# Chunked attention and a two-layer block in one kernel: dense weights, whole turns, grouped scores and values, transposes by the DMA crossbar, and W1 scaled in place

## The chip, the core and the metric

The kernel runs on one core of a Trainium2 chip. The core has a matrix engine (TensorE, PE in the profile; its weight loads are the row PEld), a vector engine (VectorE, DVE), a scalar engine (ScalarE, ACT), GpSimd (POOL) and a queue for transfers (SyncE, SP). TensorE writes to PSUM, eight banks of 2 KB per partition; the other engines copy from there to SBUF. Transfers are issued by an engine's queue and carried out by 16 DMA engines. The metric is device microseconds of one execution; lower is better. Each engine works through its own instructions in order and waits where an input is not there.

## What is computed

Four batches of eight heads, 768 positions, head width 64. Each chunk of 32 queries looks at 8 memory keys, up to 16 keys before the chunk, its own 32 and 8 behind. The heads side by side give 512 numbers per position, and on these runs a normalised two-layer block with a residual:

```python
k_full = np.concatenate([mem_k, k_ctx], axis=2)
v_full = np.concatenate([mem_v, v_ctx], axis=2)
scores = scale * np.matmul(q_c, k_full.transpose(0, 1, 3, 2))
scores = scores - np.max(scores, axis=-1, keepdims=True)
a = np.exp(scores)
a = a / (np.sum(a, axis=-1, keepdims=True) + 1e-09)
out[:, :, c_start:c_end] = np.matmul(a, v_full)
...
xn = (x - mu) / np.sqrt(var + 1e-06) * g_ln
ch = np.maximum(xn @ w_ch1, 0.0) @ w_ch2
return (x + ch).astype(np.float32)
```

w_ch1 is 512 x 2048, w_ch2 is 2048 x 512.

## The kernel before

Work is cut into 24 tiles of 128 positions (tile t is batch t // 6) and 12 pairs of tiles (pair u is tiles 2u and 2u+1). A tile is four chunks of 32 queries: two groups (`gg`) of 64, each with two chunks (`y`). For one tile the attention goes like this, with the lines of the profile:

- `qk` (L313): `qk_products` makes 32 small products (L294) in one PSUM bank. Each has 64 contraction rows (one head; two heads, `par`, lie in the two halves of the partitions), 32 queries and 64 keys. `below_max` (L304, L305, DVE) takes off the row maximum, `weights` (L311, ACT) the exponential into `P`.
- `pt` (L317): four TensorE transposes (L321) turn `P`, and two copies (L330), first DVE for one half of the partitions and then ACT for the other, put it into `PTz`. There each half of the partitions (keys of chunk y) holds only its own chunk's queries; the other places are zeros, set once.
- `val` (L367): `val_products` has 16 products (L336) of 128 contraction rows, 64 queries and 65 columns (values and a column of ones) in the two banks `two`. The zeros make one product serve both chunks. `tokens` (L345, L346, L352, DVE) divides by the sum and gives the mean; `shift` (L359 on POOL, L363 on ACT in the first six tiles) takes the mean off into `xn`.
- `root` (L374 on ACT, L378 and L382 on POOL) makes the inverse deviation `rstd`, used only at the end, when the result is added.
- `turn_x` (L388): four TensorE transposes of `xn`; a DVE copy (L394) multiplies by `g` on the way into `xT`.

For a pair, `up` (L407) has eight blocks of 8 products of 256 columns, each block followed by a ReLU copy (L415 on ACT) into `rT`. The second layer is `down` (L423, eight blocks of four products of 512 columns) in pairs 0 and 1, and from pair 2 on `down7` (L472): seven blocks of 8 products of 256 columns, by sums of blocks of the weights (`w2_sum`, L453, into `T`) and of `rT` (`r_sum`, L468). After each, DVE adds into `xs` (L479), and SP stores a finished tile (L433, L484).

Keys and queries of a batch come by POOL transfers into `raw`, heads apart: `turn` (L232) makes 16 narrow transposes of 96 rows for two heads, and copies (L245, L252) put the result into `KT` and `QD`. Memory keys are put into `KT` by `mem_cols`. Values come by POOL transfers straight into `V` (`load_v_group` L125 and L130 for batch 1, `load_v_head` L139 and L144 after it, `load_v_ends`); SP makes the copies inside `V` that chunks share (`v_shared` L161, `v_mem` L166).

The order is written out by hand; no scheduler moves anything. Batch 0 and pairs 0 and 1 are straight code. From pair 2 on, `plan` lists for pair u and step 0 to 15 what is put in ahead of that step's block: even steps are `up` of pair u, odd steps `down7` of pair u-1 (`down` in pair 2; none at step 15). While pair u runs, the attention of the two tiles of pair u+1 is made: scores at steps 0 and 2, `pt` at 4 and 7, `val` at 6 and 9, `turn_x` at 11 and 14 (in pair 2 all but the turns are four steps later; turns at 14 and 16). Batches 2 and 3 are turned in pairs 3 and 4, and 6 and 7, four turns a pair, at steps 8, 9, 12 and 13; their loads are issued at step 5 of pairs 2 and 5.

PSUM banks that are free for turns and scores go round through `slot()`: from pair 2 on there are only two of them, `one`.

Of the kernel before, what the change touches and what calls it, by code (L numbers as in the profile page):

```python
# [9 lines left out]
FP16 = mybir.dt.float16  # L10
# [6 lines left out]
def kernel(  # L17
# [50 lines left out]
    PTz = [sb.tile([128, 16, 2, 32], FP16, name=f"PTz{i}") for i in range(3)]  # L68
# [187 lines left out]

    RAW = ((0, 1), (0, 1), (2, 0), (1, 2))

    def turn_k(b, j, engine):
        to_stream(KT[b % 2], turn(raw[RAW[b][0]], 2 * j), j, engine)  # L260

    def turn_q(b, j, engine):
        to_rows(b, turn(raw[RAW[b][1]], 2 * j), j, engine)
# [53 lines left out]
    def pt(t, engines="VA"):  # L317
# [8 lines left out]
        z = PTz[t % 3]  # L326
        src = pv.rearrange("p (c q) -> p c q", c=16)
        for y in range(2):
            rows = slice(64 * y, 64 * y + 64)
            copy_on(engines[y])(out=z[rows, :, y, :], in_=src[rows, :, :])  # L330

    def val_products(t):
        b, tt = t // 6, t % 6
        for h in range(H):
            for gg in range(2):
                nc.tensor.matmul(  # L336
                    out=two[64 * gg : 64 * gg + 64, 128 * h : 128 * h + 65],
                    lhsT=PTz[t % 3][:, 4 * (h // 2) + 2 * gg + h % 2, :, :],
                    rhs=V[b % 2][:, 2 * tt + gg, h, 0:65],
                    start=True, stop=True, tile_position=(0, 64 * gg),  # L340
                )
# [42 lines left out]
    def turn_x(t):  # L384
        p = slot()
        pv = as16(p)[:, 0:512]
        for dt in range(4):
# [6 lines left out]
        nc.vector.tensor_tensor(  # L394
            out=xT[(t // 2) % 3][:, :, 128 * i : 128 * i + 128],
            in0=pv.rearrange("p (d c) -> p d c", d=4),
            in1=free(g_col, 0, [[1, 4], [0, 128]]), op=ALU.mult,
        )

# [196 lines left out]
    for i in range(2):  # L596
        nc.vector.memset(PTz[i][64:128, :, 0, :], 0.0)
        nc.vector.memset(PTz[i][0:64, :, 1, :], 0.0)
# [10 lines left out]
    nc.vector.memset(PTz[2][64:128, :, 0, :], 0.0)  # L609
    nc.vector.memset(PTz[2][0:64, :, 1, :], 0.0)  # L610
# [29 lines left out]
    shift(1, "A")  # L640
    turn_x(0)
# [18 lines left out]
    for g in range(2):  # L660
        load_v_group(1, g)
    up(0, 3)
# [16 lines left out]
    v_turn(7, "A")  # L679
    up(0, 4)  # L680
# [34 lines left out]
    banks["list"] = one + upb  # L715
    down(0, 0)
    val(5, "A")
    turn_x(4)
    down(0, 1)
    mem_cols(KT[1], memKT[:, 4:8, :], True)  # L720
    down(0, 2)
    turn_x(5)
    down(0, 3)
    root(4)
    for g in range(6, 9):
        load_v_group(1, g)
    turn_k(1, 0, "V")
    down(0, 4)
    root(5)
    for g in range(9, NG):  # L730
        load_v_group(1, g)
    turn_k(1, 1, "A")
    down(0, 5)
    turn_k(1, 2, "V")
    down(0, 6)
    turn_k(1, 3, "A")
# [12 lines left out]
    for j in range(4):  # L749
        at(2, j, turn_q, 1, j, "AV"[j % 2])  # L750
    for u in range(2, NP - 1):
        a, c = 2 * u + 2, 2 * u + 3
        d = 4 if u == 2 else 0
        at(u, d, qk, a)
        at(u, d + 2, qk, c)
        at(u, d + 4, pt, a)
        at(u, d + 6, val, a)
        at(u, d + 7, pt, c)
        at(u, d + 9, val, c)
        if u == 2:  # L760
            at(u, 14, turn_x, a)
            at(u, 15, root, a)
            at(u, 16, turn_x, c)
            at(u, 16, root, c)
        else:
            at(u, 11, turn_x, a)
            at(u, 12, root, a)
            at(u, 14, turn_x, c)
            at(u, 14, root, c)
# [4 lines left out]
    for b in range(2, B):  # L774
        u0 = 3 * b - 3
        at(u0 - 1, 5, load_kq, b)
        for j in range(4):
            w, s = u0 + j // 2, 8 if j % 2 == 0 else 12
            at(w, s, turn_k, b, j, "V")
            at(w, s + 1, turn_q, b, j, "A")  # L780
        for h in range(H):
            for part in range(2):
                at(u0, 2 * h, load_v_head, b, h, part)
        at(u0 + 1, 0, load_v_ends, b)
        at(u0 + 1, 8, v_shared, b, 0, NG)
# [58 lines left out]
```

## Time and profile before

| What | Value |
| --- | --- |
| Runs | 255.0, 256.27, 256.6 us; median 256.27 |
| Profiled execution, first to last instruction (span) | 255.3 us; the page gives no other time for it |
| Mean granted TensorE clock | 0.971 |
| Busy: PE, DVE, ACT, POOL | 235.8, 176.0, 122.0, 94.4 us |
| Start, to the first `up` of pair 0 | 28.7 us |
| Pair 0; 1; 2 | 22.4; 19.0; 19.1 us |
| Pairs 3, 4, 5, 6 | 19.1, 19.05, 16.15, 18.6 us |
| Pairs 7, 8, 9, 10 | 19.0, 16.1, 16.6, 16.7 us |
| Pair 11 and the last `down7` | 20.4 us |
| Last stores | 4.3 us |

The page has busy times per engine, a strip of the span in 40 slices, the chain of work that ended last, groups of instructions by line, and transfers by name. Beside it the trace was read in order of time and by stretches. In the order of time a row is: start, length, engine, line, operation, output<-inputs, tile sizes, count, and in brackets how long the engine stood idle before it and for whom. PE products overlap, so a row's length is more than its share; the distance from one start to the next is what counts.

### The profile page before, as it was taken

What the parts mean: (1) busy time and instruction counts of PE and PEld (TensorE: products, weight loads), DVE (VectorE), ACT (ScalarE), POOL (GpSimd) and SP (SyncE); (2) the same over time, 40 slices, a digit from 0 to 9 for tenths busy, and PEclk for the clock granted to TensorE, in tenths of its full rate; (3) what the DMA queues carried; (4) which work ended last, traced back from release to release, by engine and by line L of the source; (5) the groups of instructions that cost most, each with busy time, mean ns of one, the idle gap of its engine ahead of it and who ended that gap; (6) DMA issues with size and microseconds to landing.
All of it is one profiled execution on the core that took longest, in us unless ns stands there. A gap on an engine that the chain in (4) does not pass through costs nothing.

```text
span 255.3 us, 8286 instructions
## 1 busy us (share of the span) xinstructions
PE 235.8 (92%) x3611; PEld 192.9 (76%) x3611; DVE 176.0 (69%) x390; ACT 122.0 (48%) x226; POOL 94.4 (37%) x164
## 2 busy tenths in 40 slices
PE   8697978999999989999999999999999999999983
PEld 7353656786566778888789878878889888899972
DVE  7535574757597598697696687687775966856272
ACT  2225456578345445545644464554555444653310
POOL 8394332016991296741322638712113022121000
PEclk9959995999999999999999999999999999999999
DMA  6989999932999987974196569933101002011022
GB/s 82 139 94 207 208 215 206 202 27 17 60 172 143 198 103 46 103 101 70 65 155 114 104 42 58 135 70 61 57 3 51 34 3 82 3 43 43 3 82 83
DMA packets 45816, 23.50 MB, mean 92 GB/s; under 512 B 33492, under 2 KB 41140, under 8 KB 45732
## 3 DMA queue, kind: packets, MB, share of 16 engines
q0 software_dynamic: 40672, 14.70, 49.2%
q1 hardware_dynamic: 5108, 8.28, 11.1%
q8 instruction: 28, 0.46, 0.8%
q14 instruction: 8, 0.07, 0.1%
HBM read 29.46 MB, written 6.29 MB: 140 GB/s over the span
## 4 chain that ended last, share of the span: by engine, by line
PE 69%; DVE 18%; ACT 4%; DMA 4%; issue 3%; DVEq 0%; ACTq 0%; POOLq 0%
PE upb L407 28%; PE dnb L472 18%; PE dnb L423 5%; DVE RS L468 4%; PE one L232 4%; DMA raw<-in_k_dram 4%; PE two L336 4%; DVE nmx L304 3%; DVE sub L305 3%; DVE xs L479 3%; PE one L294 2%; PE one L388 2%; ACT PTz L330 2%; PE upb L542 2%; DVE T L453 1%
## 5 line engine op out<-in xcount | busy, mean ns | idle before, releaser
L407 PE MATMUL upb<-xT,w1c 128*128 128x256 f16 x768 | 101.3, 276 | 1.2 <-DVE xT L394 0.9
L407 PEld LDWEIGHTS <-w1c 128*128 128x128 f16 x768 | 80.0, 115 | 5.5 <-DVE xT L394 1.4
L415 ACT ACTIVATE rT<-upb 128x512 f16<-128x512 f32 x92 | 54.6, 593 | 56.9 <-PE upb L407 56.7
L479 DVE SCALAR_TENSOR_TENSOR xs<-dnb,rstd,xs 128x256 f32<-128x256 f32 x70 | 33.7, 481 | 24.3 <-PE dnb L472 23.1
L359 POOL TENSOR_SCALAR xn<-xs,nmean 128x512 f16<-128x512 f32 x18 | 12.4, 691 | 76.6 <-DVE nmean L352 36.8
L472 PEld LDWEIGHTS <-RS 128*128 128x128 f16 x320 | 30.0, 98 | 4.3 <-DVE RS L468 0.7
L311 ACT ACTIVATE P<-sub 128x512 f16<-128x512 f32 x24 | 15.2, 632 | 35.0 <-DVE sub L305 34.9
L472 PE MATMUL dnb<-T,RS 128*128 128x256 f16 x240 | 30.9, 273 | 0.8 <-DVE xs L479 0.8
L472 PEld LDWEIGHTS <-rT 128*128 128x128 f16 x240 | 23.1, 98 | 2.6
L472 PE MATMUL dnb<-w2c,rT 128*128 128x256 f16 x160 | 20.6, 273 | 0.0
L394 DVE TENSOR_TENSOR xT<-one,g_col 128x512 f16<-128x512 f16 x22 | 15.1, 687 | 7.4 <-PE one L388 7.2
L232 PEld LDWEIGHTS <-raw 96*64 96x64 f16 (+2 forms) x576 | 13.5, 110 | 8.6 <-issue 5.8
L378 POOL TENSOR_SCALAR veps<-ssq 128x1 f32<-128x1 f32 x24 | 5.4, 227 | 36.2 <-ACT sq L374 36.0
L374 ACT ACTIVATE sq<-xs,nmean 128x512 f16<-128x512 f32 x24 | 17.3, 719 | 0.2
L346 DVE CUSTOM_DVE_ANT_1 xs<-two,rec 128x512 f32<-128x512 f32 x24 | 16.6, 691 | 0.8
L468 DVE TENSOR_TENSOR RS<-rT 128x1024 f16<-128x1024 f16 x20 | 13.7, 686 | 4.9 <-ACT rT L415 4.9
L423 PE MATMUL dnb<-w2c,rT 128*128 128x512 f16 x64 | 16.3, 380 | 0.0
L336 PEld LDWEIGHTS <-PTz 128*64 128x64 f16 x384 | 8.5, 114 | 10.2 <-ACT PTz L330 6.0
L304 DVE TENSOR_REDUCE nmx<-one 128x8 f32<-128x512 f32 x21 | 14.4, 684 | 2.1 <-PE one L294 2.0
L305 DVE TENSOR_TENSOR sub<-one,nmx 128x512 f32<-128x512 f32 x21 | 14.5, 691 | 0.7
L336 PE MATMUL two<-V,PTz 128*64 128x65 f16 x384 | 11.1, 202 | 4.1 <-ACT PTz L330 3.3
L382 POOL TENSOR_TENSOR rstd<-veps,mhalf 128x1 f32<-128x1 f32 x24 | 13.3, 554 | 2.0
(118 smaller groups left out, 321.4 us busy)
## 6 DMA issues: line engine op xcount, KB each, us to landing
out_dram<-xs SPq DMA_DIRECT2D x23, 256.0 KB, 2.0
raw<-in_k_dram POOLq DMA_DIRECT2D x4, 768.0 KB, 9.8
raw<-in_q_dram POOLq DMA_DIRECT2D x3, 768.0 KB, 14.8
w1c<-in_moe_w_ch_dram POOLq DMA_DIRECT2D x2, 1024.0 KB, 13.3
w2c<-in_moe_w_ch_dram POOLq DMA_DIRECT2D x4, 512.0 KB, 22.7
V<-in_v_dram POOLq DMA_DIRECT2D x16, 77.0 KB, 3.1
V<-in_v_dram POOLq DMA_DIRECT2D x15, 56.0 KB, 4.1
V<-memv SPq DMA_DIRECT2D x6, 120.0 KB
```

The costliest lines, as they stand in the source:

```text
L232: nc.tensor.matmul(out=pv[64 * par : 64 * par + 64, n * r : n * r + n], lhsT=src[lo : lo + n, heads + par, r, :], rhs=identity[lo : lo + n ...
L304: nc.vector.tensor_reduce(out=m, in_=scores, axis=AX.X, op=ALU.max)
L305: nc.vector.tensor_tensor(out=s.rearrange("p (c k) -> p c k", c=8), in0=scores, in1=free(m, 0, [[1, 8], [0, 64]]), op=ALU.subtract,)
L336: nc.tensor.matmul(out=two[64 * gg : 64 * gg + 64, 128 * h : 128 * h + 65], lhsT=PTz[t % 3][:, 4 * (h // 2) + 2 * gg + h % 2, :, :], rhs=V ...
L346: nc.vector.tensor_tensor_reduce(out=x.rearrange("p (h d) -> p h d", h=H), in0=free(two, 0, [[128, 8], [1, 64]]), in1=free(r, 0, [[1, 8], ...
L374: nc.scalar.activation(out=sq, in_=xs[t % 9], func=ACTF.Square, bias=nmean[t % 6], scale=1.0, accum_out=ssq[i],)
L407: nc.tensor.matmul(out=p[:, 256 * hb : 256 * hb + 256], lhsT=free(w1c[hc // 8][:, dt, :], 512 * (hc // 4 % 2) + hc % 4, [[4, 128]]), rhs=x ...
L415: nc.scalar.activation(out=o, in_=i, func=ACTF.Relu)
L423: nc.tensor.matmul(out=p, lhsT=rT[u % 2][:, hc, 128 * i : 128 * i + 128], rhs=w2c[hc // 4][:, hc % 4, :], start=(hc == 0), stop=(hc == 15),)
L468: nc.vector.tensor_tensor(out=RS[k], in0=a, in1=b, op=op)
L472: nc.tensor.matmul(out=p[:, 0:256], lhsT=left[:, n, :], rhs=right(n), start=(n == 0 and not add), stop=(n == 7), skip_group_check=add,)
L479: nc.vector.scalar_tensor_tensor(out=x, in0=p[:, 0:256], scalar=rstd[t % 9], in1=x, op0=ALU.mult, op1=ALU.add,)
```

## The change

- **Dense weights.** `PTz` is replaced by `PT`, the turned weights as they are. One copy by ACT instead of two halves. `val_products` makes 32 products of 64 contraction rows and 32 queries, each half of the partitions by itself.
- **Whole turns.** From batch 1 on, POOL's new `mix` copies two heads side by side (96 x 1024), and `turn_mixed` turns 96 x 128 in 8 products instead of 16. Keys and queries of batch 1 are turned in pair 1 (one query turn in pair 2), those of batches 2 and 3 all in pairs 3 and 6; their loads are issued at step 0 of the pair before.
- **Crossbar.** From tile 8 on, weights and tokens are turned by transposing DMAs on SP's queue: `cross_p` from `P` to `PT` (no PSUM, no copy), `cross_x` from `xn` to `xT`.
- **Grouping.** From pair 3 on, `val` of tile t and the scores of tile t+2 stand together, at steps 4 and 8; `cross_x` at 6 and 10, `cross_p` at 7 and 11, `root` at 7 and 11.
- **W1 times g.** `scale_w1` multiplies W1 by `g` in place, in eight passes of 128 x 1024 (five on DVE, three on ACT); the copy after `turn_x` is a plain one.
- **Moved.** `w2_sum` 0 and 1 to pair 1, 2 and 3 to steps 7 and 9 of pair 2; `mem_cols` of batches 1 to 3 earlier; V loads of batches 2 and 3 from step 0 to step 6 of pairs 3 and 6 on, and the V copies two steps later.

```diff
-    PTz = [sb.tile([128, 16, 2, 32], FP16, name=f"PTz{i}") for i in range(3)]
+    PT = [sb.tile([128, 4, 128], FP16, name=f"PT{i}") for i in range(3)]
+    mixed = [sb.tile([128, 8, 128], FP16, name=f"mixed{i}") for i in range(4)]
...
+    def mix(b, which, j):
+        src, m = raw[RAW[b][which]], mixed[(2 * j + which) % 4]
+        nc.gpsimd.tensor_copy(
+            out=m[0:96, :, :].rearrange("p r (a d) -> p r a d", a=2),
+            in_=free(src[0:96], 1024 * j, [[64, 8], [512, 2], [1, 64]]),
+        )
+    def turn_mixed(which, j):
+        p, src = slot(), mixed[(2 * j + which) % 4]
+        pv = as16(p)
+        for r in range(8):
+            nc.tensor.matmul(
+                out=pv[:, 96 * r : 96 * r + 96], lhsT=src[0:96, r, :],
+                rhs=identity[0:96, 0:96], is_transpose=True, start=True, stop=True,
+            )
+        return pv
...
-        z = PTz[t % 3]
-        src = pv.rearrange("p (c q) -> p c q", c=16)
-        for y in range(2):
-            rows = slice(64 * y, 64 * y + 64)
-            copy_on(engines[y])(out=z[rows, :, y, :], in_=src[rows, :, :])
+        copy_on(engine)(out=PT[t % 3].rearrange("p j q -> p (j q)"), in_=pv)
...
-                nc.tensor.matmul(
-                    out=two[64 * gg : 64 * gg + 64, 128 * h : 128 * h + 65],
-                    lhsT=PTz[t % 3][:, 4 * (h // 2) + 2 * gg + h % 2, :, :],
-                    rhs=V[b % 2][:, 2 * tt + gg, h, 0:65],
-                    start=True, stop=True, tile_position=(0, 64 * gg),
-                )
+                for y in range(2):
+                    rows, col = slice(64 * y, 64 * y + 64), 64 * gg + 32 * y
+                    q0 = 64 * gg + 32 * (h % 2)
+                    nc.tensor.matmul(
+                        out=two[col : col + 32, 128 * h : 128 * h + 65],
+                        lhsT=PT[t % 3][rows, h // 2, q0 : q0 + 32],
+                        rhs=V[b % 2][rows, 2 * tt + gg, h, 0:65],
+                        start=True, stop=True, tile_position=(64 * y, col),
+                    )
...
+    def cross_x(t):
+        i = t % 2
+        nc.sync.dma_start_transpose(
+            out=xT[(t // 2) % 3][:, :, 128 * i : 128 * i + 128], in_=xn[t % 3],
+        )
+    def cross_p(t):
+        nc.sync.dma_start_transpose(out=PT[t % 3], in_=P[t % 3])
+    def scale_w1(c, dt, engine):
+        w = w1c[c][:, dt, :]
+        if engine == "A":
+            nc.scalar.activation(out=w, in_=w, func=ACTF.Copy, scale=g_col[:, dt : dt + 1])
+        else:
+            nc.vector.tensor_scalar(
+                out=w, in0=w, scalar1=g_col[:, dt : dt + 1], scalar2=None, op0=ALU.mult,
+            )
...
     shift(1, "A")
+    for dt in range(4):
+        scale_w1(0, dt, "AV"[dt // 2])
     turn_x(0)
...
     v_turn(7, "A")
+    for dt in range(4):
+        scale_w1(1, dt, "VVVA"[dt])
     up(0, 4)
...
+            for step, t in ((4, a), (8, c)):
+                at(u, step, val, t)
+                if t + 2 < 2 * NP:
+                    at(u, step, qk, t + 2)
+            at(u, 7, root, a)
+            at(u, 11, root, c)
+            at(u, 6, cross_x, a)
+            if u < NP - 2:
+                at(u, 7, cross_p, a + 2)
+            at(u, 10, cross_x, c)
+            if u < NP - 2:
+                at(u, 11, cross_p, c + 2)
...
-        at(u0 - 1, 5, load_kq, b)
+        at(u0 - 1, 0, load_kq, b)
+        for n, (j, which) in enumerate((j, w) for j in range(4) for w in range(2)):
+            w, step = ((-1, 12), (-1, 13), (0, 0), (0, 1), (0, 3), (0, 5), (0, 6), (0, 7))[n]
+            at(u0 + w, step, mix, b, which, j)
+            step = (1, 2, 5, 6, 10, 11, 13, 15)[n]
...
         for h in range(H):
+            w, step = divmod(6 + 2 * h, 16)
             for part in range(2):
-                at(u0, 2 * h, load_v_head, b, h, part)
+                at(u0 + w, step + part, load_v_head, b, h, part)
```

## The prediction

> **What bounds the kernel now.** I read the page's busy times, clock row and chain first, then TensorE in order of time, then the stages, then DMA and POOL. Busy share, clock and chain agree:
>
> ```profile
> PE 235.8 (92%) x3611; PEld 192.9 (76%) x3611; DVE 176.0 (69%) x390; ACT 122.0 (48%) x226; POOL 94.4 (37%) x164
> ...
> PEclk9959995999999999999999999999999999999999
> ...
> PE 69%; DVE 18%; ACT 4%; DMA 4%; issue 3%; DVEq 0%; ACTq 0%; POOLq 0%
> ```
>
> TensorE is full from 28.7 us to the tail at full clock, except near 38 to 45 us (tenth 5). So from pair 1 on, a microsecond of TensorE work is a microsecond of time, unless another engine is late. What one block costs is the distance between starts in the order of time (ends are modelled), here inside pair 7:
>
> ```profile
> 162.14 0.41 PE L294 MATMUL one<-KT,QD 64*32 64x64 f16 x32
> 162.48 1.07 PE L407 MATMUL upb<-xT,w1c 128*128 128x256 f16 x8
> 163.39 1.04 PE L472 MATMUL dnb<-w2c,rT 128*128 128x256 f16 x8
> ...
> 166.47 0.39 PE L321 MATMUL one<-identity,P 128*128 128x128 f16 x4
> 166.70 1.04 PE L407 MATMUL upb<-xT,w1c 128*128 128x256 f16 x8
> 167.57 1.04 PE L472 MATMUL dnb<-T,RS 128*128 128x256 f16 x8
> 169.19 0.44 PE L336 MATMUL two<-V,PTz 128*64 128x65 f16 x16 [0.58 <-ACT PTz L330]
> 169.56 1.07 PE L407 MATMUL upb<-xT,w1c 128*128 128x256 f16 x8
> 170.47 0.39 PE L321 MATMUL one<-identity,P 128*128 128x128 f16 x4
> 170.69 1.04 PE L472 MATMUL dnb<-T,RS 128*128 128x256 f16 x8
> 171.66 0.53 PE L232 MATMUL one<-identity,raw 96*64 96x96 f16 x16
> 172.12 1.07 PE L407 MATMUL upb<-xT,w1c 128*128 128x256 f16 x8
> ```
>
> An `up` or `down7` block takes 0.87 (166.70 to 167.57); turning the weights 0.23 (166.47 to 166.70), the tokens 0.22. Scores take 0.35 and values 0.37, but a full-array block ahead of such a narrow one takes 0.97, and the block behind 0.91: changing the shape costs 0.14, so 0.49 and 0.51. A narrow turn takes 0.46 + 0.13 = 0.59. In the row at 169.19 values also wait 0.58 for ACT's half of the weights' copy, which starts only after DVE's half. The stages:
>
> ```profile
> 89.20:108.30 19.10, 18.11 (x298) 15.56 (x296) 15.56 (x33) 10.42 (x21) 14.38 (x24) 1.00 0.86 85
> ...
> 162.14:181.18 19.04, 18.13 (x297) 15.57 (x296) 14.76 (x35) 10.18 (x19) 5.92 (x11) 1.00 0.44 73
> 181.18:197.30 16.12, 15.94 (x232) 14.28 (x232) 12.14 (x28) 8.09 (x16) 2.56 (x7) 1.00 0.09 34
> ```
>
> (Stretch and its length, then busy PE, PEld, DVE, ACT, POOL, clock, DMA.) Pairs with turns take about 19 us, those without 16 to 16.7; pairs 3 to 10, 89.2 to 230.6, together 141.4.
>
> **Pairs 3 to 10.** Old contents per pair: 15 blocks x 0.87 = 13.1, two scores 0.98, two values 1.02, two weight and two token turns 0.90; sixteen narrow turns lie in pairs 3, 4, 6, 7. That is 8 x 16.0 + 16 x 0.59 = 137.4; the other 4.0 are waits like the 0.58 above and the 0.94 for xT at 90.56. The change:
> - Turns of weights and tokens leave TensorE for tiles 8 to 23: 16 x 0.45 = -7.2.
> - Whole turns: 8 products of 96 columns instead of 16. Scaled from the 128-column turn (0.23 for four), 0.34; at the same time per product, 0.46. I take 0.38, with no change of shape: 16 x 0.21 = -3.4.
> - Values: 32 products instead of 16, each half as tall and half as wide. The scores have just this form (64 rows, 32 columns, two row halves into one bank) and run at 0.34/32 = 11 ns, so 0.35 against 0.37: I take nothing. Upper end: 23 ns each, as the old values ran, +0.37 a tile.
> - Grouping: values and the next-but-one scores stand together in one shape, 14 changes of 0.14 gone: -2.0; two scores move to pair 2: -0.7.
> - The 4.0 of waits: weights are now ready a pair early and the end-of-pair token turn is gone. All go, if the crossbar is in time.
>
> Sum -17.3, so 124.1 for the eight pairs.
>
> **The crossbar's deadline.** Values of the second tile are at step 8, and the next pair's first `up` needs both tiles' xT. Between lie scores 0.45 and seven blocks 6.1: 6.55 us. From the end of values to the end of the shift on POOL the trace has 2.1 (values end 134.44, xn 135.83 + 0.69). Leaves 4.4 for a transpose of 128 KB, issued by SP. The trace has none. Lower end: the same queue's stores:
>
> ```profile
> out_dram<-xs SPq DMA_DIRECT2D x23, 256.0 KB, 2.0
> ...
> out_dram<-xs SPq DMA_DIRECT2D x2, 128.0 KB, 1.7
> ...
> q0 software_dynamic: 40672, 14.70, 49.2%
> ```
>
> Upper end: the software queue's pieces, mostly under 512 B, cost 0.492 x 16 x 255.3 / 40672 = 49 ns of an engine. The result has 512 runs of 256 B: 512 x 49 / 16 = 1.6 us on top of 1.7, so 3.3. Cut eight times finer it is 12.5 + 1.7 = 14. I take 3.3, nearest to the stores: hidden, with 1.1 to spare. Past 4.4 every microsecond costs eight (pairs 4 to 11). The weights' transposes have a pair of slack, except the first two, which stand on SP behind pair 1's stores; these go out about 1 us into pair 3, and values 8 need them 4.3 us into it: 3.3 just fits. On SP each transpose waits for its input with stores and the V copies queued behind it; those stores are waited for only at the end.
>
> The Trainium skill, "Advanced Engine Details and Errata", section X-Bar Transpose (TRN2), calls transposes as fast as regular DMAs: by it the price is the store's 1.7, and the sum stays. No run here shows it yet.
>
> **POOL.** It gets 24 `mix` copies of 96x1024. Rates: its 128x1536 memset took 1.40 (0.93 for 1024), its shift 0.69 per 512 (1.38). I take 1.2. It is one queue, in order:
> - Pair 1: POOL issues the V loads back to back from 62.4 to 77.8. Four mixes put in there add 4.8 us; the third key turn (about 65.5) needs one that comes after the loads of groups 3 to 5 (66.3 + 1.2). Wait: 1.5 (0 to 3).
> - The loads of keys and queries of batch 2 slip with it from 76.3 and 77.1 to 81 and 82. Queries took 14.8 us to land: 96.7, plus a mix 97.9; the first query turn would run at about 94.9. Wait: +3.0 (0 to 5). Scores, shifts and V loads behind that mix slip as well. In batch 3 the loads are issued at the start of pair 5 and took 7.2 and 10.5, 12 us ahead of need: nothing.
> - In pair 3, six mixes, one shift, a root and two V loads stand ahead of the second shift, some 11 us of POOL against 10 us of TensorE: shift 1.2 late, but there four turns lengthen the deadline by 1.5. Nothing.
>
> **DVE and ACT.** DVE loses 24 half copies of 0.41 and 16 token copies of 0.69; per turn pair it has about 15.4 of 18 us, so no bound. After values it makes tokens (1.2), then maximum and difference (1.3): the bank of scores is free 2.7 us after the values, about when the query turn of step 6 wants it: nothing.
>
> **Scaling W1.** Eight in-place passes of 128x1024, not in the trace; ACT: 0.777 per 768, so 1.0; DVE: between 0.69 (128x1024 subtraction) and 0.91 (memset), lower if a one-input copy (0.48 per 1280) is nearer; I take 0.6. At the start: the weights' copy is one of 0.58 instead of 0.41 then 0.58, -0.5; two ACT passes behind the second shift (ends 27.5) end at 29.5 less that 0.5, and the first block's second product needs them, against 28.73: +0.8. Net +0.3. Before `up(0,4)` (42.43): ACT is free of the V copy at 44.2, then its pass to 45.2, and the block's fourth product needs it: the half-clock block ends some 2.5 later, of which token work that was late there anyway gives back 0.5: +2.0 (0 to 3). The memsets that go are hidden behind the first key load.
>
> **Pairs 1 and 2.** In pair 1 seven whole turns of 0.38 replace four of 0.59: +0.3. In pair 2 one replaces four: -2.0; two more scores +0.98, one change less -0.14: -1.1.
>
> **Sum.** +0.3 + 2.0 + (0.3 + 1.5) - 1.1 - 17.3 + 3.0 = -11.3. The profiled span of 255.3 becomes 244.0. The page shows no time beside the span; runs were 255.0 to 256.6, median 256.27, so about 1.0 lies around it: **245.0 us**.
>
> **Rivals.**
> - Slower, the crossbar is late. Decides from 4.4 us; break-even at 4.4 + 11.3/8 = 5.8. At 8 us, (8 - 4.4) x 8 = 29: 274. For: no transpose in the trace, and small pieces are dear here. Against: it moves half a store's bytes. 0.18, and 0.12 for 4.4 to 5.8 us, 245 to 256.
> - POOL becomes the bound: a mix takes 2.4 instead of 1.2. The second shift of pairs 3 and 6 comes some 7 us later, of which 1 is covered: +6 each, and +5 before batch 2: 262. Against: POOL's rows give 1.38 at most. 0.06.
> - Values don't speed up in parallel tiles, so halving does not pay: 24 x 0.37 = 8.9: 253.9. 0.06. Against: the scores' 11 ns in the same form and bank. The Trainium skill, "TensorEngine Tiling (Array Packing)", Gotcha 1: PSUM Pressure, says that different row tiles cannot access one PSUM bank at the same time; by that rule the halves would run in turn. The scores' rows speak against it.
> - The forecast, 238 to 250: 0.58.
>
> 1% is 2.6 us, about what a measurement of this kernel can tell from no change. Faster 0.58 + 0.07 + 0.03 = 0.68; within 1% 0.05 + 0.03 = 0.08; slower 0.18 + 0.06 = 0.24. Range: best ends of start, pair 0, pair 1 and the batch-2 wait (-0.5, 0, 0.3, 0) with turns at 0.34 give 236; upward it takes most of the late-crossbar case in: 272.
>
> **What would show it.** Pairs 4, 5, 7, 8, 9 of about 14.8 us; values at 0.35; waits of `up` for a transpose absent; a wait of the first query turn of pair 3 for POOL's mix of about 3; `up(0,4)` some 2.5 late behind ACT's scaling. Wrong if a transpose takes over 5 us from issue to landing, if mixes take over 1.6, or if values stay at 23 ns a product.

## The result

The changed kernel takes 262.53 us (261.31 to 268.36) against 255.63 (253.85 to 256.6) for the kernel before on the same chip: 1.026 times as long, 95% interval 1.020 to 1.031. The forecast was 245.0, faster.

Some executions ran in a slower state of the chip: medians are over all of them, ratios leave the slow ones out, and the profiles of `e2`, `e9`, `e11` and `e12`, which are of slow ones, are read for waits and order, not for time.

The page of the changed kernel, with the lines that answer to those shown of before (busy time, granted clock, chain):

```profile
PE 229.8 (88%) x3675; PEld 190.6 (73%) x3675; DVE 156.6 (60%) x347; ACT 113.8 (44%) x215; POOL 121.2 (46%) x188
...
PEclk9858995599999997999997699999999999999999
...
PE 45%; DMA 19%; POOL 11%; DVE 8%; ACT 8%; issue 5%; SPq 2%; POOLq 0%; DVEq 0%; ACTq 0%
```

TensorE has less work, as forecast, but its share of the chain that ended last fell from 69 to 45%, and DMA's rose from 4 to 19%. The clock row has new dents near 100 and near 143 us (tenths 7, and 7 and 6). What TensorE waited for, summed over the run, with the number of waits and the longest:

```profile
PE two L356 <- DMA V<-memv: 10.5, 5, 5.5
PE one L271 <- POOL mixed L261: 3.3, 2, 2.1
PE upb L444 <- DMA xT<-xn: 2.3, 2, 1.6
```

The values (L356) wait 10.5 us for the memory rows of V, a wait that the kernel before does not have. The stages of pairs 3 to 10 (stretch and its length, then busy PE, PEld, DVE, ACT, POOL, clock, DMA):

```profile
94.75:118.03 23.28, 19.44 (x313) 16.78 (x312) 17.24 (x38) 11.00 (x21) 18.44 (x25) 0.93 0.69 78
118.03:132.70 14.67, 14.67 (x248) 13.44 (x249) 9.27 (x22) 6.34 (x13) 9.68 (x17) 1.00 1.20 136
132.70:155.90 23.20, 17.21 (x251) 14.76 (x250) 10.40 (x23) 7.04 (x14) 4.43 (x9) 0.85 0.98 144
155.90:175.72 19.82, 17.67 (x315) 16.18 (x314) 16.28 (x32) 10.13 (x19) 17.04 (x22) 1.00 0.49 60
175.72:190.40 14.68, 14.68 (x248) 13.46 (x249) 10.15 (x26) 6.58 (x14) 10.02 (x17) 1.00 1.20 129
190.40:208.10 17.70, 14.88 (x250) 13.51 (x249) 10.31 (x23) 6.93 (x14) 2.85 (x6) 1.00 0.51 103
```

Pairs without a long wait (4 and 7, also 9), called undisturbed below, take 14.7 us, against 16 to 19 before: the forecast's 14.8. Pair 5 holds most of the loss (8.4 us over the forecast); pairs 3, 6 and 8 are 2.5, 2.0 and 2.9 over it. Against the forecast, stage by stage:

| Stage | Forecast | Measured |
| --- | --- | --- |
| Start, to the first `up` | 29.0 | 28.7 |
| Pairs 0 and 1 | 45.2 | 46.8 |
| Pair 2 | 18.0 | 19.3 |
| Pairs 3 to 10 | 127.1 | 142.1 |
| Pair 11 and after it, stores | 24.7 | 24.0 |
| Span | 244.0 | 260.9 |

So 15.0 of the 16.9 us lie in pairs 3 to 10. TensorE in order of time, inside pair 5:

```profile
136.86 0.19 PE L356 MATMUL two<-V,PT 64*32 64x65 f16 x1 [0.48 <-DMA V<-memv]
142.56 0.62 PE L356 MATMUL two<-V,PT 64*32 64x65 f16 x31 [5.51 <-DMA V<-memv]
...
143.54 1.90 PE L444 MATMUL upb<-xT,w1c 128*128 128x256 f16 x8
145.23 1.92 PE L509 MATMUL dnb<-T,RS 128*128 128x256 f16 x8
```

The pair is 8.5 us longer than pair 4: 6.0 of waiting, and some 2.5 of slow clock behind it (0.85 in this pair's row). The next two blocks take 1.69 and 1.70 from start to start instead of 0.87, the one after them 1.16, and the values and scores at the end of the wait are stretched too. What SP and POOL had issued before that (SP's rows, then POOL's):

```profile
128.53 1.19 SPq L421 DMA_TRANSPOSE xT<-xn  x1
130.01 0.79 SPq L162 DMA_DIRECT2D V<-V  x1
130.85 2.34 SPq L167 DMA_DIRECT2D V<-memv  x2
```

```profile
132.09 0.84 POOL L118 DMA_DIRECT2D raw<-in_k_dram  x1
132.92 0.77 POOL L118 DMA_DIRECT2D raw<-in_q_dram  x1
```

The memory rows go out at 130.85, POOL's 1.5 MB of keys and queries of batch 3 1.2 us behind them, and the values want the rows at 136.4, 5.5 us after their issue. They get the last of them at 142.5. The load is not all of it. In pair 8, where POOL issues no load of keys and queries any more, the same rows still take 8.0 us (issued at 188.99, there at 197.0), and the values wait 2.8 for them:

```profile
188.99 2.34 SPq L167 DMA_DIRECT2D V<-memv  x2
```

```profile
197.07 0.42 PE L356 MATMUL two<-V,PT 64*32 64x65 f16 x31 [2.04 <-DMA V<-memv]
```

The copies are as late as that because they follow V's loads and, on SP, the second tile's transpose (128.53), which waits for the shift. POOL issues the first of V's loads at 107.72, 13.0 us into pair 3. Before, it was 91.74, 2.5 us into pair 3; the same copies and the same load were 14 us apart, and the values came 20 us after the copies:

```profile
112.78 0.76 SPq L161 DMA_DIRECT2D V<-V  x1
113.59 2.35 SPq L166 DMA_DIRECT2D V<-memv  x2
```

```profile
127.38 0.84 POOL L117 DMA_DIRECT2D raw<-in_k_dram  x1
...
134.00 0.44 PE L336 MATMUL two<-V,PTz 128*64 128x65 f16 x16 [0.18 <-ACT PTz L330]
```

(The last row is TensorE's.) The chain that ended last names the four transfers that the end hung on in pairs 3 to 8 (start, length):

```profile
112.23 5.67 DMA xT<-xn
...
131.64 10.88 DMA V<-memv
...
170.81 4.77 DMA xT<-xn
...
189.75 7.27 DMA V<-memv
```

### The profile page after: what moved, and what is told of

It reads as the page before. It is cut to its first block, busy times and chain, and to the rows that moved or that the text cites. A ratio compares the mean times of both kernels' runs of the same rounds, so it can differ in the third digit from the quotient of the medians.

```text
span 260.9 us, 8465 instructions
## 1 busy us (share of the span) xinstructions
PE 229.8 (88%) x3675; PEld 190.6 (73%) x3675; DVE 156.6 (60%) x347; ACT 113.8 (44%) x215; POOL 121.2 (46%) x188
## 2 busy tenths in 40 slices
DMA packets 63224, 27.70 MB, mean 106 GB/s; under 512 B 50900, under 2 KB 58548, under 8 KB 63140
## 3 DMA queue, kind: packets, MB, share of 16 engines
q1 hardware_dynamic: 22516, 12.48, 22.1%
## 4 chain that ended last, share of the span: by engine, by line
PE 45%; DMA 19%; POOL 11%; DVE 8%; ACT 8%; issue 5%; SPq 2%; POOLq 0%; DVEq 0%; ACTq 0%
PE upb L444 20%; PE dnb L509 14%; DMA V<-memv 7%; DMA raw<-in_q_dram 5%; DMA xT<-xn 4%; DMA raw<-in_k_dram 3%; POOL mixed L261 3%; PE upb L579 3%; POOL V L126 2%; PE two L356 2%; POOL V L131 2%; DVE xs L366 2%; ACT rT L452 2%; ACT sq L394 2%; PE dnb L233 1%
## 5 line engine op out<-in xcount | busy, mean ns | idle before, releaser
L444 PE MATMUL upb<-xT,w1c 128*128 128x256 f16 x768 | 103.1, 280 | 4.4 <-DMA xT<-xn 2.3
L444 PEld LDWEIGHTS <-w1c 128*128 128x128 f16 x768 | 82.5, 116 | 11.3 <-issue 2.6
L452 ACT ACTIVATE rT<-upb 128x512 f16<-128x512 f32 x92 | 53.3, 593 | 48.0 <-PE upb L444 47.9
L509 PEld LDWEIGHTS <-RS 128*128 128x128 f16 x320 | 31.5, 99 | 4.5 <-DVE RS L505 0.7
L379 POOL TENSOR_SCALAR xn<-xs,nmean 128x512 f16<-128x512 f32 x18 | 13.7, 763 | 41.3 <-DVE nmean L372 41.2
L261 POOL COPY mixed<-raw 96x1024 f16<-96x1024 f16 x24 | 26.5, 1135 | 10.9 <-DMA raw<-in_k_dram 5.6
L356 PE MATMUL two<-V,PT 64*32 64x65 f16 x768 | 11.7, 198 | 11.2 <-DMA V<-memv 10.5
L356 PEld LDWEIGHTS <-PT 64*32 64x32 f16 x768 | 8.2, 97 | 17.5 <-DMA V<-memv 9.6
L505 DVE TENSOR_TENSOR RS<-rT 128x1024 f16<-128x1024 f16 x20 | 14.9, 746 | 8.5 <-ACT rT L452 8.5
L365 DVE RECIPROCAL rec<-two 128x8 f32<-128x8 f32 x24 | 4.8, 202 | 20.0 <-PE two L356 19.9
L271 PEld LDWEIGHTS <-mixed 96*128 96x128 f16 x192 | 10.5, 97 | 7.4 <-POOL mixed L261 4.1
## 6 DMA issues: line engine op xcount, KB each, us to landing
raw<-in_q_dram POOLq DMA_DIRECT2D x3, 768.0 KB, 14.8
```

The lines of the kernel that those rows point to most:

```text
L261: nc.gpsimd.tensor_copy(out=m[0:96, :, :].rearrange("p r (a d) -> p r a d", a=2), in_=free(src[0:96], 1024 * j, [[64, 8], [512, 2], [1, 64]]),
L356: nc.tensor.matmul(out=two[col : col + 32, 128 * h : 128 * h + 65], lhsT=PT[t % 3][rows, h // 2, q0 : q0 + 32], rhs=V[b % 2][rows, 2 * tt ...
L444: nc.tensor.matmul(out=p[:, 256 * hb : 256 * hb + 256], lhsT=free(w1c[hc // 8][:, dt, :], 512 * (hc // 4 % 2) + hc % 4, [[4, 128]]), rhs=x ...
L452: nc.scalar.activation(out=o, in_=i, func=ACTF.Relu)
L505: nc.vector.tensor_tensor(out=RS[k], in0=a, in1=b, op=op)
L509: nc.tensor.matmul(out=p[:, 0:256], lhsT=left[:, n, :], rhs=right(n), start=(n == 0 and not add), stop=(n == 7), skip_group_check=add,)
```

## The experiments

Theory A after the result: V's copies, which the change put two steps later while it put the values two steps earlier, reach the values too late, and the rest is the transposes that stand among them on SP. Rivals: POOL's loads slow whatever is issued beside them, so that a wait taken away comes back elsewhere (B); the scaling of W1 costs more than reckoned (C); the crossbar itself is a bad exchange for TensorE's turns (D). Each is a ratio to the kernel before, on the same chip:

| Kernel | Median us | Ratio, 95% interval |
| --- | --- | --- |
| the change | 262.53 | 1.026 (1.020 to 1.031) |
| e1, memory rows early | 255.02 | 0.998 (0.991 to 1.006) |
| e2, loads at step 5 | 264.08 | 1.016 (1.006 to 1.026) |
| e3, no scaling | 261.03 | 1.022 (1.016 to 1.029) |
| e4, turns on TensorE | 261.80 | 1.026 (1.020 to 1.032) |
| e5, memory rows a pair early | 258.99 | 1.016 (1.010 to 1.022) |
| e6, e5 and second tile on TensorE | 250.90 | 0.985 (0.980 to 0.990) |
| e7, e5 and queries before V | 262.24 | 1.028 (1.021 to 1.035) |
| e8, three repairs and scaling early | 250.66 | 0.985 (0.979 to 0.990) |
| e9, memory rows behind transposes | 252.06 | 0.983 (0.972 to 0.994) |
| e10, queries between V's groups | 245.84 | 0.962 (0.953 to 0.970) |
| e11, all tokens on TensorE | 252.57 | 0.986 (0.972 to 0.999) |
| e12, second tile alone | 257.06 | 1.003 (0.997 to 1.009) |
| e13, e9 and V's loads behind transposes | 259.01 | 1.016 (1.008 to 1.024) |
| e14, e10 with e13's loads and the second tile by the crossbar | 250.89 | 0.981 (0.974 to 0.989) |
| e15, e10 without the crossbar | 260.20 | 1.022 (1.013 to 1.032) |

### Memory rows early (e1)

```diff
-        at(u0 + 1, 10, v_mem, b)
+        at(u0, 8, v_mem, b)
...
     up(0, 7, "V")
+    v_mem(1)
...
-    at(2, 0, v_mem, 1)
```

> The changed kernel, with only the memory rows of V (v_mem) issued earlier: batch 1 at the end of pair 0, batches 2 and 3 at step 8 of pairs 3 and 6 instead of step 10 of pairs 4 and 7; the shared rows (v_shared) stay. Theory A (values wait for V copies that the change made late: 1.7 us in pair 2, 6.0 in pair 5, 2.8 in pair 8, and some 2.4 of half clock behind the long one): if the memory rows, last on SP's queue, are what is late, about 12 us go: 250. Rival (the shared rows ahead of them are just as late): not more than 3 us go, 260, and the waits are then named for V<-V. In either case the waits of up for xT in pairs 3 and 6 stay.

Measured 255.0, 7.5 below the change. No wait of the values for a memory row is left, but `up` now waits for transposes, 8.4 us instead of 2.3:

```profile
PE upb L444 <- DMA xT<-xn: 8.4, 3, 4.1
```

In its chain of work the transposes of the second tiles of pairs 3 and 6 take 8.13 and 7.11 us instead of 5.67 and 4.77; SP had issued the memory rows two steps ahead of each. So A is right on the first wait, and what took its place stands in SP's order too, or beside POOL's loads.

### The loads at step 5 (e2)

```diff
-        at(u0 - 1, 0, load_kq, b)
+        at(u0 - 1, 5, load_kq, b)
```

> The changed kernel, with the loads of keys and queries of batches 2 and 3 back at step 5 of the pair before. Theory A1 (the 1.5 MB of these loads, issued right behind the V copies at 131 to 133 us, are what stretches the copies from some 5 us in pair 7 to 10 in pair 4): the wait of values in pair 5 falls from 6.0 to about 3 and the half clock behind it goes, 257.5. Rival (the copies are slow by themselves or late by their place in SP's queue): the wait stays at 5 to 6, 262.5. The first turns of pair 6 may then wait up to 2 us for the loads.

The wait of pair 5 for V's rows fell from 6.0 to 2.3 us, so the load beside the rows carried most of that wait. The rest is there without it: the rows took 8.0 us (131.74 to 139.8), as in pair 8 of the change, and not the 5 or so that the expectation starts from. But then `up` of pair 6 waited 4.9 us for its tokens, whose transpose now stood beside the load. Ratio 1.016 instead of 1.026, with intervals that overlap: as B has it, the load moves the wait, and a transposing DMA is as exposed as a copy.

### No scaling (e3)

```diff
-    for dt in range(4):
-        scale_w1(0, dt, "AV"[dt // 2])
...
-    for dt in range(4):
-        scale_w1(1, dt, "VVVA"[dt])
```

> The changed kernel without scale_w1: W1 is not multiplied by g, so the output lacks the factor g; all else the same. Theory B (the two sets of scaling passes hold up the first block of pair 0 by 0.9 us and the fifth by 3, since the passes stand ahead of what TensorE waits for): 258.5. Rival (what holds up pair 0 is the slow clock and the attention chain of tiles 2 and 3): 262.

Ratio 1.022, 1.5 us in the medians and within the intervals. V's waits stay at 10.5, and pair 3's wait for the mix grows to 3.3. C falls as a main cause.

### Turns on TensorE (e4)

```diff
-            at(3, 0, cross_p, a + 2)
-            at(3, 0, cross_p, c + 2)
+            at(3, 0, pt, a + 2)
+            at(3, 0, pt, c + 2)
...
-            at(u, 6, cross_x, a)
+            at(u, 9, turn_x, a)
...
-                at(u, 7, cross_p, a + 2)
+                at(u, 9, pt, a + 2)
...
-            at(u, 10, cross_x, c)
+            at(u, 13, turn_x, c)
...
-                at(u, 11, cross_p, c + 2)
+                at(u, 13, pt, c + 2)
```

> The changed kernel with the crossbar undone: weights and tokens of tiles 8 to 23 turned by TensorE and copied by ACT and DVE as in tiles 0 to 7, tokens at steps 9 and 13, weights at 9 and 13. Theory C (the crossbar did what was forecast: 16 x 0.45 = 7.2 us of TensorE saved, against 2.4 of waits for xT): 262.5 + 7.2 - 2.4 = 267, less up to 2 because the longer pairs cover part of the wait for the V copies. Rival (the crossbar's transposes crowd the queue and are the cause of the loss): 258 or less, with the waits of values for V copies gone.

The same time as the change. The waits for V fall to 1.0 us (in pair 2) with no V copy moved in the program: with no transpose ahead of them on SP, the memory rows of batch 2 go out 4.4 us ahead of POOL's load (130.26) and 9.5 ahead of the values' want (135.4), instead of 1.2 and 5.5:

```profile
125.86 2.35 SPq L167 DMA_DIRECT2D V<-memv  x2
```

About half of this is that the pairs are longer (POOL issues V's last load 8.2 us ahead of pair 5 instead of 6.1), the other half that SP's queue is free when the loads are there. So V's late loads alone do not make the wait of pair 5; the transposes ahead of the copies have a part in it. The waits for xT go as well, but the transposes of the weights now wait in each pair for the bank that the scores still hold, and 32 more turns are on TensorE:

```profile
PE one L342 <- DVE sub L326: 8.3, 7, 1.3
```

So as the change stands, the crossbar saves nothing: what it takes off TensorE goes into the waits that it causes and undergoes. That does not tell what it would be worth without them (e15).

### Memory rows a pair early, and in what order (e5, e9)

```diff
...
-        at(u0 + 1, 10, v_mem, b)
+        at(u0 - 1, 9, v_mem, b)     # e5: ahead of cross_x of step 10
+        at(u0 - 1, 12, v_mem, b)    # e9: behind it
```

> The changed kernel with the memory rows of V written a pair earlier than in the run with the memory rows early (step 9 of pairs 2 and 5 instead of step 8 of pairs 3 and 6; batch 1's as there, after up(0,7)), so that SP issues nothing but transposes, one shared copy and the output stores in the pair that ends with a wait for a transpose. Theory: in that run the transposes were late because they stood behind the two memory-row copies, which had been put two steps ahead of them; the waits of up for a transpose fall from 8.4 us in all to the 2.3 of the changed kernel, and the time from 255.0 to about 249. Rival: the transposes are late because of POOL's loads beside them, and the waits for the values had merely hidden it; then the waits stay near 8 and the time near 255.

> As the run with the memory rows of V a pair early, but at step 12 of pairs 2 and 5 instead of step 9, so that SP issues them behind the second tile's transposes of steps 10 and 11 and not right ahead of them. In that run the transpose of tile 11's tokens (pair 5) landed 10.4 us after its issue began, 1.1 us behind the memory rows and with the load of batch 3's keys and queries going on, and up(6,0) waited 6.0 us; in the run with the memory rows early the transposes that came late were those of pairs 3 and 6, where the rows stood at step 8. Theory: it is the order on SP and its DMA rings; the wait of up(6,0) falls to 1 us or less, and the time from 259.0 to about 252. Rival: it is the load of batch 3; the wait stays at 4 us or more, and the time at 257 to 259.

e5 came out slower than e1, against its theory, and its trace says why: the rows now stood right ahead of a transpose, but in pair 5, where the load of batch 3 goes on too. SP's rows, then the chain:

```profile
142.93 1.48 SPq L167 DMA_DIRECT2D V<-memv  x2
145.50 2.52 SPq L421 DMA_TRANSPOSE xT<-xn  x1
```

```profile
145.50 10.43 DMA xT<-xn
```

A transpose that lands in 2.7 us by the median of the change's page took 10.4, and `up(6,0)` waited 6.0. e9 changes only the order:

```profile
145.10 1.19 SPq L421 DMA_TRANSPOSE xT<-xn  x1
...
148.27 1.48 SPq L167 DMA_DIRECT2D V<-memv  x2
```

```profile
150.87 1.06 PE L444 MATMUL upb<-xT,w1c 128*128 128x256 f16 x8 [1.29 <-DMA xT<-xn]
```

The transpose is there after 5.7 us, the wait is 1.3, and the ratio goes from 1.016 to 0.983. The order on SP was 4.7 us of that wait and its shadow in the clock; 5.7 where 2.5 would do is what stays. With this one repair (the memory rows of all batches early, and behind the transposes), and all of the crossbar left as the change has it, the changed kernel beats the kernel before.

### The second tile on TensorE, with the rows early and alone (e6, e12)

```diff
-            at(u, 10, cross_x, c)
+            at(u, 13, turn_x, c)        # e6 on top of e5; e12 alone
```

> As the run with the memory rows a pair early, and the tokens of the second tile of each pair from 3 on are turned by TensorE at step 13, as before, instead of by the crossbar at step 10; first tiles and weights stay with the crossbar. The turn adds four products of 0.06 us a pair, some 2 us in all of eight pairs. Theory: no up waits for a transpose any more, neither at a full nor at a halved clock afterwards; 247 to 250, below the run with the memory rows a pair early by what waits that run still has, less 2. Rival: what is late is the shift (xn) itself, on POOL behind a mix; then TensorE waits for it at step 13 or just behind it, and nothing is gained: 253 to 257.

> The changed kernel with one edit: the tokens of the second tile of pairs 3 to 10 are turned by TensorE at step 13; the V copies stay where the change put them. Theory: the two faults are separate. The waits for V's memory rows stay at 9 to 11 us in all, those of up for a transpose (2.3 us) go and about 2 us of products come: 260 to 263, against 258.99 with the V copies alone and 250.9 with both. Rival: the transposes and the V copies hold each other up in SP's queue; with fewer transposes the V waits fall by half too: 255 to 258.

e6: 250.9, no wait of `up` for a transposing DMA. It equals e9 (0.985 and 0.983): where the rows stand right, no difference can be told between the second tile turned by TensorE and by the crossbar. e12: the theory of two separate faults falls. With the V copies left late, their waits fall from 10.5 to 5.8 us, now that one transpose (and its wait for the shift) no longer stands ahead of them on SP:

```profile
128.11 2.35 SPq L167 DMA_DIRECT2D V<-memv  x2
```

They go out 2.1 us ahead of POOL's load (130.22) instead of 1.2, and 6.8 us instead of 5.5 ahead of the values' first want; the wait in pair 5 is 1.9 instead of 6.0, though the weights' transpose, which SP issued behind the rows, now brings 1.9 of its own there. That it is the head start on the load which counts is argued from these times; no run measured it apart.

### Queries, scaling, loads (e7, e8, e10)

```diff
+    load_kq(2)                      # e7, e8: before V's groups 6 to 11
     for g in range(6, 9):
         load_v_group(1, g)
...
+    load_kq(2)                      # e10: between groups 8 and 9
     for g in range(9, NG):
         load_v_group(1, g)
```

> As the run with the memory rows a pair early, and the keys and queries of batch 2 are loaded before V's groups 6 to 11 of batch 1 instead of at step 0 of pair 2. Theory: the queries land some 9 us earlier, so that the first query turn of pair 3 no longer waits for POOL's mix (2 to 3 us, and TensorE's clock halved for some 2 us behind it): 3 to 4 below the run with the memory rows a pair early. Rival: the V groups, now behind 1.5 MB, come late for V's shared copies of batch 1 at steps 1 and 2 of pair 2 and stop SP, with the weights' transposes of pair 3 behind them: no gain, or a loss of 2 to 5.

> All of the last three (memory rows a pair early, second tiles turned by TensorE, queries before V's groups), and the second half of W1 is multiplied by g before pt(3) and val(2) instead of after them, which takes the waits of up(0,4) for it (1.3 us) if its load has landed by then. Theory: the costs are separate waits and add: 242 to 247, below both kernels. Rival: a wait removed in one pair is given back in the next, since the loads on POOL pace pairs 2 to 8: 249 to 254.

> As the run with all of the last three, but batch 2's keys and queries are loaded between V's groups 8 and 9 of batch 1, not before group 6 (there POOL's issues of the last groups waited 7.1 us, SP's shared copies took 16.4 us with that, and the two weights' transposes of pair 3 came 2.3 us late), and those two weights (tiles 8 and 9) are turned by TensorE. Theory: the wait for the transposes of tiles 8 and 9 goes (2.3 us and the halved clock behind it) and the tokens of pair 2 come on time: 246 to 248. Rival: each of these waits is only the visible end of loads that pace pairs 2 and 3; the time stays at 250 to 251.

e7's rival came true. Its mix was on time, but POOL's next V loads waited for the queue's big loads, SP's shared copies of V waited for them, and the two weights' transposes of pair 3 stood behind those on SP. The same in e8 (SP's rows):

```profile
76.12 16.35 SPq L162 DMA_DIRECT2D V<-V  x3
...
97.42 4.67 SPq L426 DMA_TRANSPOSE PT<-P  x2
```

so that e8 gained nothing on e6. e10 is e8 with two edits, which no run separates: it turns those two weights by TensorE and puts the load between the groups. Its page:

```profile
PE 226.6 (93%) x3715; PEld 190.2 (78%) x3715; DVE 159.4 (65%) x355; ACT 114.5 (47%) x217; POOL 122.7 (50%) x188
...
PEclk9989995999979999999999999999999999999999
...
PE 63%; DMA 16%; POOL 8%; issue 5%; DVE 5%; ACT 1%; POOLq 0%; DVEq 0%; ACTq 0%
```

245.84 us, 0.962 (0.953 to 0.970): 3.8% below the kernel before, 6.2% below the change. One wait of 4.8 us is left, in pair 1 for POOL's mix. Its transposes land no sooner than the change's (its page gives medians of 5.7 us for weights and 4.4 for tokens, the change's 2.4 and 2.7), but nothing waits for one. Pairs 4 to 6:

```profile
112.96:127.87 14.91, 14.91 (x256) 13.68 (x254) 10.89 (x27) 7.42 (x15) 11.40 (x20) 1.00 1.17 113
127.87:142.77 14.90, 14.90 (x254) 13.71 (x253) 10.64 (x24) 6.94 (x14) 4.41 (x8) 1.00 1.22 178
142.77:161.88 19.11, 18.06 (x319) 16.40 (x318) 16.07 (x32) 9.25 (x18) 16.34 (x21) 1.00 0.76 92
```

Pairs 5 and 8 (14.90 each) are as long as pair 4: 0.23 over the change's undisturbed 14.67, the 0.22 to 0.23 of one turn by TensorE put back.

### All tokens on TensorE, and no crossbar (e11, e15)

```diff
+            at(u, 9, turn_x, a)         # e11: on top of e6; e15: on top of e10
...
+                at(u, 9, pt, a + 2)     # e15 only
+                at(u, 13, pt, c + 2)    # e15 only
```

> As the run with the second tile's tokens on TensorE (250.9 us), with the first tile's tokens turned by TensorE too (step 9): only the weights go by the crossbar. It adds four products a pair, some 0.25 us at the undisturbed clock, and a copy on VectorE of some 0.3 us, eight times. Theory: the crossbar pays for first tiles, which have 10 steps to spare; about 2 us slower, 252 to 254. Rival: with fewer transposes on SP and no transposed tokens behind the weights, nothing is lost: 250 to 251.

> As the run with queries between V's groups (245.84 us), with everything turned by TensorE: weights and tokens of both tiles, at steps 9 and 13. It tells what the crossbar is worth once nothing is late. Theory: the turns cost what they cost in the run with all turns on TensorE, some 0.6 us a pair of products and 1.2 us a pair of waits for the score bank; 252 to 258, so the crossbar is worth 6 or more. Rival: with V, queries and W1 on time the turns fall into waits that are there anyway; 246 to 249.

e11's interval takes in e6: the first tile's turn makes no difference that could be told. e15 is 14 us slower than e10, and slower than the kernel before. Its undisturbed pairs take 16.8 us against 14.9:

```profile
201.00:217.80 16.80, 15.65 (x267) 14.38 (x265) 11.06 (x25) 8.05 (x17) 2.85 (x6) 1.00 0.09 34
```

Of these 1.9, 0.75 are three turns of some 0.25, and 1.15 the wait for the scores' bank (as in e4), which is due to where this kernel puts `pt`, right behind scores. With the turns placed better one would still pay for the 22 turns of some 0.25 that e10 leaves to the crossbar, 5.5 us; that is an estimate from these rows, and was not tried. So D falls: the crossbar is worth 14 us against the turns as this kernel places them, and by the estimate 5 or 6 against better placed ones, once nothing is late.

### V's loads out of the transposes' way (e13, e14)

```diff
-            w, step = divmod(6 + 2 * h, 16)
+            w, step = divmod(11 + h, 16)
             for part in range(2):
-                at(u0 + w, step + part, load_v_head, b, h, part)
+                at(u0 + w, step, load_v_head, b, h, part)
```

> As the run with the memory rows of V behind the transposes (252.06 us), and POOL issues V's loads of batches 2 and 3 from step 11 of pairs 3 and 6 to step 2 of the next pair, two a step, instead of from step 6 to step 5 of the next, one a step; the tokens' transposes of steps 6 and 10 then stand before these loads and after none. In that run the transposes that up waited for in pairs 4 and 7 landed 5.7 and 5.1 us after their issue, with V's loads going on. Theory: the loads stretch them; they land in 2.4 to 3.5 us, the waits of up for them (1.7 and 1.0 us) go, and some 2 to 4 us with them: 248 to 250. Rival: they are late because the token shift on POOL stands behind a mix, or they are slow in themselves in these pairs; landing times stay at 4.5 us or more and the time at 251 to 254.

> As the run with queries between V's groups (245.84 us), with V's loads behind the transposes as in the run before this one, the memory rows at step 12, and the second tile's tokens turned by the crossbar again as in the changed kernel. Theory: with nothing beside them the transposes of second tiles are on time, and eight turns of some 0.25 us leave TensorE: 243 to 245. Rival: transposes of second tiles still come late in pairs 3 to 6; 247 to 250, so that TensorE's turn is the better for them.

In e13 the waits of `up` at the end of pairs 3 and 6 (1.69 and 0.96 in e9) are gone, as B says; the tokens' transpose of pair 3 is there 4.7 us after its issue at the latest, instead of 5.7. Short waits (0.8 and 1.0) come at the end of pairs 4 and 7 instead. And the loads now stand later in the pair, the shared copy of V behind them too: it goes out (130.91) 0.6 us behind POOL's load of batch 3 (130.34), where in e9 it was 2.1 ahead of that load (130.78 and 132.85), and the values of pair 5 wait longer than all that was won:

```profile
130.91 9.34 DMA V<-V
...
140.38 0.63 PE L356 MATMUL two<-V,PT 64*32 64x65 f16 x32 [4.78 <-DMA V<-V]
```

(The first row is the chain's, the second TensorE's.) 259.0 instead of 252.1. In e14 the transpose of pair 3 still took 5.05 us, with V's loads starting 2.8 us behind it as in e13, so how much of the 5 to 6 us the loads make stays open. It is 5 us slower than e10 and has 3.6 us of waits of `up` for transposes, which e10 does not have. Since it also moves V's loads and the memory rows, it does not show by itself that the second tile's turn is better left to TensorE; beside e6 and e9, which differ in that turn and in the step of the rows, no difference was told.

## Why the prediction was wrong

**The step that failed** is one that was not made: the V copies got no deadline. The prediction saw that "each transpose waits for its input with stores and the V copies queued behind it" and then went on to the stores alone, which are waited for only at the end. The change's own list moves the copies two steps later and the values two steps earlier; V's loads start 10 us later in their pair, the memory rows stand on SP behind the shared copy that waits for these loads, and from the rows' issue to the values' want there are then 5.5 us, against 20 before. They needed 11.7 with POOL's load beside them (130.85 to 142.5), and 8.0 without one (pair 8, e2), so they would have been late by 2.5 even by themselves. The crossbar has its part in it: the rows stand on SP behind the second tile's transpose and its wait for the shift, and in e4, with no transposes there and longer pairs, pair 5 does not wait. Measured: 1.7, 6.0 and 2.8 us in pairs 2, 5 and 8, and some 2.5 of half clock: 13 of the 16.9 us that the forecast missed. By the runs, moving the memory rows alone (e9) takes 10.5 us away, 1.026 to 0.983; e9 still waits for transposes and for the mix, which is where the rest of the 13 seems to come back.

**The crossbar's deadline** (taken 3.3 us, 4.4 allowed, break-even 5.8): by the page's medians it lands in 2.4 to 2.7, better than taken:

```profile
PT<-P SPq DMA_TRANSPOSE x16, 2.4
xT<-xn SPq DMA_TRANSPOSE x16, 2.7
```

but it is not one number: 4.8 and 5.7 us in pairs 6 and 3, with V's loads going on (past the 5 us that the prediction named as a sign of being wrong), 10.4 behind V's rows and beside a load (e5). The bounds 1.7 to 14 held; the multiplier did not: only two of eight pairs were late, so the rival "crossbar late, times eight" is not what happened either. The Trainium skill, "Advanced Engine Details and Errata", section X-Bar Transpose (TRN2), makes transposes as fast as regular DMAs. The medians come near that and no more: 2.4 and 2.7 for 128 KB, beside 2.9 for this run's stores of 256 KB and the 1.7 that the prediction took from the 128 KB stores before. What the forecast does not have is what traffic beside them does.

**Pairs 0 to 2**: the wait for the scaled W1 before `up(0,4)` was 1.3 and half-clock blocks behind it, near the 2.0; pairs 0 and 1 together cost 5.4 instead of 3.8. Pair 2 came out 1.3 over its forecast, with 1.7 us of waits for V in it.

**POOL**: a mix took 1.14 (1.03 by itself; taken 1.2). The wait of the first query turn of pair 3 was 2.1 and half a clock behind it, for the 3.0 forecast. The clock's share was never in the sum, here or at V's waits. In pair 6 a query turn waited 1.4 for the bank of scores that DVE's subtraction still held, a wait that the prediction had put at nothing.

**Right**: pairs 4, 7 and 9 at 14.7 (14.8); values at 0.35 (in pair 10 of e10, where no scores follow, from 210.18 to the next block at 210.53), 11 ns a product, with two row halves writing different partitions of one PSUM bank; a whole turn 0.34 (0.38); two shapes grouped. The Trainium skill, "TensorEngine Tiling (Array Packing)", Gotcha 1: PSUM Pressure, has row tiles on one PSUM bank unable to access it at the same time; these rows show no loss from that in this form. That e10 comes to 245.84 beside the forecast of 245.0 is in part chance, since it makes ten turns more on TensorE than forecast and orders loads and copies otherwise; but its undisturbed pairs, 14.9, are the forecast's mechanism.

## What to carry to other kernels

When steps are moved, give every transfer that crosses them a deadline: the time from its place on its queue to its first reader, before and after, and what else is on the wire in between. A DMA that does TensorE's work is cheap only while its queue and the wire are free, so issue what must be there soon ahead of what has time, and put bulk loads between deadlines rather than beside them. And price a stall on TensorE above its length, since the clock often drops behind it.

## What the hardware showed beyond that

- Behind waits of about 2 us and more TensorE's clock was often halved for the next one or two blocks, but by no sharp rule that these runs show: waits of 1.86 (e7), 2.00 (e12), 2.04 (twice in e2), 2.13 (pair 3 of the change), 2.21 (e8) and 5.5 us were followed by at least one block of some 1.5 us or more instead of 0.87, while 2.03 (e5), 2.04 (pair 8 of the change), 2.28 (e8), 3.08 (e11) and even 3.30 us (e3) left it full. The Trainium skill, "TensorE: Matmul & The Clock Gate", section Why this matters for your kernels, allows gaps of up to about 3 us; these rows say that 2 is already a risk, and that 3 need not cost anything. The blocks behind the 2.13 of pair 3:

```profile
99.13 0.51 PE L271 MATMUL one<-identity,mixed 96*128 96x96 f16 x8 [2.13 <-POOL mixed L261]
99.48 1.68 PE L444 MATMUL upb<-xT,w1c 128*128 128x256 f16 x8
```

- A transposing DMA of 128 KB is many small pieces: the changed kernel moves 22516 packets on its hardware queue with 32 transposes, e10 17076 with 22, so 544 each, and the count of packets under 512 B differs by the same 5440 (50900 and 45460). That it suffers so from traffic beside it fits this, but was not tested apart.
- VectorE's fp16 subtractions of 128x1024 took 0.68 in all cases before; in the changed kernel six of them, each beside a POOL mix, took 0.95 to 1.41, and the mean of the group that the page lists rose to 0.75:

```profile
96.01 0.68 DVE L505 TENSOR_TENSOR RS<-rT 128x1024 f16<-128x1024 f16 x1
...
98.66 0.95 DVE L505 TENSOR_TENSOR RS<-rT 128x1024 f16<-128x1024 f16 x1
105.79 1.08 DVE L505 TENSOR_TENSOR RS<-rT,RS 128x1024 f16<-128x1024 f16 x1
```

  The mixes beside these ran at 98.04 and from 105.29 on. No wait of TensorE for these sums is in its list, so it cost little or nothing here.
